# Landmark attention and two feed-forward blocks: V' as eight 64-row tiles, the cosine as one shifted sine, 204 moved deadlines

## The chip, the cores and the metric

The kernel runs on one core of a Trainium2 chip. The core has a matrix engine (TensorE, in the profile PE, with its weight loads as PEld), a vector engine (DVE), an activation engine (ACT), GpSimd (POOL) and a sync engine (SP) whose queue issues the transfers between the chip's memory and SBUF. Matrix products land in PSUM, eight banks of 2 KB in each of 128 partitions; ACT and DVE read it. The metric is the device time of one execution in microseconds (us). TensorE's clock has two levels, 1.2 and 2.4 GHz; the profile's column PEclk gives the granted clock as a share of the higher one.

## The reference

Landmark attention over 4 batches of 8 heads (sequence 576, head size 64, 32 landmarks), then two feed-forward blocks on the 2304 x 512 result:

```python
A  = sm(q, k_lm);  Bm = sm(q_lm, k_lm);  C = sm(q_lm, k)      # sm: scaled scores, softmax
Z  = Bm.T / (norm_1(Bm) * norm_inf(Bm) + 1e-6)
for _ in range(6):
    Z = 2 * Z - Z @ Bm @ Z
x = (A @ Z @ C @ v)                    # heads side by side: [2304, 512]
h = x @ w_in;    g = h * cos(h);       x = g @ w_out           # 512 -> 2048 -> 512
h = x @ w_in2;   g = max(h, 0) + alpha * min(h, 0);  y = g @ w_out2
```

The weights arrive as 64-bit floats; the kernel takes them in as pairs of 32-bit words and rebuilds 32-bit floats on DVE.

## The kernel before, in words

**Attention.** A unit (function `unit`) works on four heads of a batch: loads of k, q and v, transposes on TensorE, landmark sums, scores, softmax. Its result `ah[b, c]` is A transposed, 128 rows (4 heads of 32 landmarks) by 576 columns, split in a high and a low part. `z_path` runs the iteration for Z of two units and ends with W, the 64 x 32 matrix of each of the eight heads by which the first feed-forward weight is folded into the landmarks: V' = W^T w_in, so that h = A V'. W goes through `put` (DVE, L857) into tile `w_`, spread with a mask so that the two heads of a 128-row pair stand in a block diagonal.

**V'.** `vprime(b, fb, c)` makes, for batch b, a slab of 512 of the 2048 columns (fb) and four of the heads (c), one tile of 128 x 512: two products of 128 rows by 64 columns (L885) with 512 streamed columns, into one PSUM bank of the pair called `x`; ACT copies it out (L887, the high part), DVE subtracts for the low part (L888). There are 4 x 4 x 2 = 32 calls. Each 32-bit product stands in the trace as two matmul records.

**Ticks.** `tick(s)` makes a block of 128 rows of h for half a batch (288 columns): 6 matmuls h (L925) into one of two banks `h`; ACT rounds h/2pi to a whole number (L930); DVE forms u = h/2pi - k (L932); ACT takes sin(pi u) (L934) and squares it (L935); DVE forms (1 - 2 sin^2) h (L936), which frees the bank; ACT copies the high part (L939), POOL or DVE subtracts (L323); 12 matmuls (L952) add it to the four `acc` banks. There are 128 ticks.

**Second block.** `btick` does the second feed-forward block, with Strassen products (L1238, L1283) and the closing products (L1319).

**The order** is not written by hand. Every operation is handed to `Plan` with the engines that can do it, a guessed duration and a deadline (`target`); deadlines run backwards through what depends on what. `go` then simulates a run and issues, again and again, the operation that can start earliest, with a small term for the deadline, and the order that it issues is each engine's program:

```python
key = s + KA * min(dl - s, KC)          # KA = 0.004
```

`s` is the planned start and `dl` the deadline, so an offset of 2 us on a deadline moves the key by 0.008 us: it decides only between operations that could start at practically the same moment. `KN` holds the constants, among them PB and AB (a bias for giving work to POOL or ACT) and SW (for switching ACT's function table). `ADJ` adds an offset to a deadline by name: `t105` is every operation of tick 105, `t112:10` its tenth, `y:13` the thirteenth of every `y_load`; u and U are units, z the iteration, v and V are V' calls, c weight conversions, e moves of y1, s, y and o loads of the second block, b its ticks. In the kernel before it is empty. The transfers go into SP's queue in the planned order too, and that queue issues one after the other.

Of the kernel before, what the change touches and what calls it, by code (L numbers as in the profile page):

```python
# [15 lines left out]

WINDOW, WARM = 3.4133, 1.275
INV2PI = 1.0 / (2.0 * math.pi)
KN = dict(T0=46, TA=3.4, TBT=3.05, VE=4.0, U1=-1, U2=36, U3=66, UD=7, UZ=20, C2=48, CD=3.0, LA=4, SW=6.0, BL=0.9, PB=0.2, AB=0.2, LM=126, JG=8, VG=8, AG=8, LW=4, LG=4, KA=0.004, KC=25, DRY=0)

ADJ = {}


class Buf:
# [17 lines left out]
class Plan:  # L42
# [71 lines left out]
    def go(self, free):  # L114
# [9 lines left out]
        for o in self.ops:  # L124
            o.dl += sum(ADJ.get(x, 0.0) for x in o.key)
        ready = {e: [] for e in free}
        seq = {t: [] for t in self.caps}
        dma_free, cur = 0.0, "exp"
        left = len(self.ops)
# [72 lines left out]
        while left:  # L202
            best = None
            for e, lst in ready.items():
                pick = None
                for o in lst:
                    sl = slots(o)
                    if sl is None:
                        continue
                    d = dict(o.engs)[e]  # L210
                    s = max(free[e], o.est, sl)
                    if e == "PE":
                        d = pe_time(s, d)
# [5 lines left out]
                    if len(o.engs) > 1 and any(  # L219
                        max(free[x], o.est, sl) + dx - BIAS.get(x, 0.0) < s + d - BIAS.get(e, 0.0)  # L220
                        for x, dx in o.engs if x != e
                    ):
                        continue
                    key = s + KA * min(dl - s, KC)
                    if pick is None or (key, dl) < pick[0]:
                        pick = ((key, dl), d, o, s)
                if pick and (best is None or pick[3] < best[3]):
                    best = (*pick, e)
            assert best is not None, "no operation can go"
            _, d, o, s, e = best  # L230
            for x, _ in o.engs:
                ready[x].remove(o)
            for b in o.bufs:
                if not b.live:
                    b.live = True
                    seq[b.tag].append(b)
                    b.t = None if KN["DRY"] else b.view(self.place[b.tag][2][(len(seq[b.tag]) - 1) % self.caps[b.tag]])
            o.eng = e
            if e == "PE":
                d = pe_time(s, o.engs[0][1], True)  # L240
            free[e] = s + d
            if o.aset:
                cur = o.aset
            if o.dma:
                dma_free = max(s + 0.65, dma_free) + o.dma
                o.end = dma_free + 0.93
            else:
                o.end = s + d
            if not KN["DRY"]:
                o.fn(e)  # L250
            work = []
            finish(o, work)
            for x in work:
                release(x)
# [4 lines left out]
def kernel(  # L259
# [12 lines left out]
    nc = tc.nc  # L272
# [156 lines left out]
    nc.vector.memset(mask, 0.0)  # L429
    for hh in range(2):  # L430
        nc.vector.memset(mask[64 * hh:64 * hh + 64, hh], 1.0)
    kq = [view([P, 2, 2, 2, M], F32)(at_kq + 32 * M * p) for p in range(NP)]
    for p in range(NP):
        nc.gpsimd.memset(kq[p], 0.0)
    g.held = dict.fromkeys("uUz", [g.buf("zf", lambda _: None)])
    alpha_sb = keep.tile([P, NF], F32, name="alpha_sb")
    kqb = [[g.buf(None) for _ in range(2)] for _ in range(NP)]
    alb = g.buf(None)

# [83 lines left out]
    def unit(u, tu):  # L523
# [72 lines left out]
        if m == 0:  # L596
# [27 lines left out]
            for hh in range(2):  # L624
                sl = slice(64 * hh, 64 * hh + 64)

                def kw(e, sl=sl, hh=hh):
                    o = kq[p][sl, :, :, hh, :]
                    i = pt.t[sl, 0:256].rearrange("p (x y b m) -> p x y b m", x=2, y=2, b=2)[:, :, 0]
                    if e == "ACT":  # L630
                        nc.scalar.activation(o, i, AF.Copy, scale=1.0 / (8.0 * SEG))
                    else:
                        nc.vector.tensor_scalar_mul(o, i, 1.0 / (8.0 * SEG))
                op([dve(128), act(128)], kw, r=[pt], w=[kqb[p][0], kqb[p][1]])
        else:
            for i, t in enumerate((kt, qt)):
# [15 lines left out]
                for hh in range(2):  # L652
                    sl = slice(64 * hh, 64 * hh + 64)

                    def kw(e, sl=sl, hh=hh, i=i, lt=lt):
                        o = kq[p][sl, i, :, hh, :]
                        x = lt.t[sl].rearrange("p (b m) -> p b m", b=2)
                        if e == "ACT":
                            nc.scalar.activation(o, x, AF.Copy, scale=1.0 / (8.0 * SEG))
                        else:  # L660
                            nc.vector.tensor_scalar_mul(o, x, 1.0 / (8.0 * SEG))
                    op([dve2(64), act(64)], kw, r=[lt], w=[kqb[p][i]])

        def scores(dst, ch, which, t, bb, pp):
            n = 64 * (CH[ch][1] - CH[ch][0])
            nc.tensor.matmul(
                out=dst.t[64 * bb:64 * bb + 64, 0:n],
                lhsT=kq[pp][:, which, bb].rearrange("p h m -> p (h m)"),
                rhs=t.t[:, CH[ch][0]:CH[ch][1], bb, :],
            )  # L670

# [85 lines left out]
    def z_path(b, tz):  # L757
# [12 lines left out]
        def pbm(e):  # L770
            for p in range(g0, g0 + n):
                for bb in range(2):
                    for hh in range(2):
                        qd = 2 * bb + hh
                        nc.tensor.matmul(
                            out=pb.t[32 * qd:32 * qd + 32, (p - g0) * M:(p - g0) * M + M],
                            lhsT=kq[p][64 * hh:64 * hh + 64, 1, bb, hh, :],
                            rhs=kq[p][64 * hh:64 * hh + 64, 0, bb, hh, :],
                        )
        op(("PE", 0.134 * n), pbm, r=[x for y in kqb[gs] for x in y], w=[pb])  # L780
        mx, bm, sm, bt = (zs(t + sx, [P, n, w]) for t, w in (("bmx", 1), ("bm", M), ("bsm", 1), ("bt", M)))
# [29 lines left out]
        def icf():  # L811
# [4 lines left out]
        vop(4, lambda e: nv.reciprocal(ic.t, ic.t), rw=[ic])  # L816
        vop(nm_, lambda e: nv.tensor_tensor(bm.t, bm.t, ic.t.to_broadcast([P, n, M]), op=ALU.mult),
            r=[ic], rw=[bm])
        w_ = sb("wt", [P, 2, P])
        c, W = cs[0], M + D  # L820
        heads = [(i, qd, slice(32 * qd, 32 * qd + 32)) for i in range(n) for qd in range(4)]

# [29 lines left out]
        op(("PE", 0.4), wm, r=[y, bm], w=pw)  # L852
        for bb in range(2):
            def put(e, bb=bb):
                o = w_.t[:, :, 64 * bb:64 * bb + 64].rearrange("p i (h m) -> p h i m", h=2)
                x = pw[bb].t[:, 0:n * M].rearrange("p (o i m) -> p o i m", o=1, i=n)
                nv.tensor_tensor(o, x.to_broadcast([P, 2, n, M]), mask.to_broadcast([P, 2, n, M]), op=ALU.mult)  # L857
            vop(128, put, r=[pw[bb]], w=[w_], target=tz)
        for i in range(2):
            wt[b, i] = w_  # L860

    vv, vload = {}, {}

    def vprime(b, fb, c, target):
        g.ctx = f"{'vV'[b > 0]}{2 * fb + c}"
        if b > 1:
            wi = []
            for p in (2 * c, 2 * c + 1):
# [4 lines left out]
                vload.setdefault((b, fb), gates["v"][0])  # L873
                wi.append(f)
        else:
            wi = [wi1[fb, 2 * c], wi1[fb, 2 * c + 1]]
        w_ = wt[b, c]
        pv = psb("x")
        d = vv[b, fb, c] = v_tile()
        valloc.append((b, fb))  # L880

        def v_mm(e):
            for bb in range(2):
                sl = slice(64 * bb, 64 * bb + 64)
                nc.tensor.matmul(out=pv.t[sl], lhsT=w_.t[:, c, sl], rhs=f32(wi[bb].t))  # L885
        op(pe(512, 4), v_mm, r=[w_, *wi], w=[pv, d], target=target)
        op(act(512, True), lambda e: nc.scalar.activation(d.t[:, 0], pv.t, AF.Copy), r=[pv], w=[d], target=target + 0.8)  # L887
        op(dve(512), lambda e: nc.vector.tensor_tensor(d.t[:, 1], pv.t, f32(d.t[:, 0]), op=ALU.subtract),  # L888
           r=[pv], rw=[d], target=target + 1.5)
# [19 lines left out]
    def tick(s):  # L909
# [9 lines left out]
        def h1_mm(e):  # L919
            i = 0  # L920
            for c in range(2):
                vh, vl = vv[b, fb, c].t[:, 0], vv[b, fb, c].t[:, 1]
                xh, xl = ah[b, c][0].t, ah[b, c][1].t
                for w_, x in ((vh, xh), (vh, xl), (vl, xh)):
# [14 lines left out]
        op(act(CW), lambda e: nc.scalar.activation(gh.t, hc.t, AF.Copy), r=[hc], w=[gh, gl])  # L939
        op([pool(CW), dve(CW)], lambda e: sub(e, gl.t, hc.t, f32(gh.t)), r=[hc, gh], w=[gl])  # L940
# [50 lines left out]

    def vgroup(b, fbs):
        for fb in fbs:
            for c in range(2):
                vprime(b, fb, c, tick_time(vfirst[b, fb]) - KN["VE"])

    FH = JG // 4
    vgroup(0, range(FH))
# [386 lines left out]
```

## Time and profile before

| what | value |
|---|---|
| median of 3 runs | 875.13 us (874.53 to 878.24) |
| profiled execution | 876.8 us, of which the span of its records is 875.0 us |
| TensorE busy | 823.1 us, 94% of the span |
| VectorE busy | 642.5 us, 73% |
| ScalarE busy | 475.9 us, 54% |
| GpSimd busy | 200.0 us, 23% |
| moved by DMA | 103.28 MB |

A busy share is an average over parts with different limits. The span has a first part in which loads and conversions feed the first ticks, a long part of ticks with the attention of later batches among them, a short change-over to the second block, and the second block itself. Where TensorE is busy all the time, the end moves only with TensorE's own work; where it waits, with what it waits for.

### The profile page before, as it was taken

Reading aid. Unit: us, or ns where it says so; the run is one execution under the profiler, and the core shown is the slowest. Engines: PE = TensorE matmul, PEld = TensorE weight load, DVE = VectorE, ACT = ScalarE, POOL = GpSimd, SP = SyncE. Lnnn points to the kernel's source line nnn. Section 1 sums busy time; section 2 is a strip of 40 time slices with the busy share of each in tenths; the row PEclk is TensorE's granted clock in tenths of the full one; section 3 lists DMA queues with packets and bytes.
Section 4 is the critical chain, followed back from the end, with each engine's and each line's share of the span. In section 5 each row is a group of like instructions: output and inputs, shape, how many; then the busy total and the mean of one; then the engine's idle time right before and its main releaser. Section 6 shows DMA issues by size and latency. Waiting matters only on the chain.

```text
span 875.0 us, 16117 instructions
## 1 busy us (share of the span) xinstructions
PE 823.1 (94%) x6065; PEld 721.5 (82%) x6065; DVE 642.5 (73%) x1296; ACT 475.9 (54%) x1085; POOL 200.0 (23%) x221
## 2 busy tenths in 40 slices
PE   6658899999999999998999889999999999999997
PEld 4337678889788878877899779899999999999996
DVE  5978979986986789777978999865665566555563
ACT  4357647787866678566876443443344324433431
POOL 0325402334431332122511332200220012000110
PEclk9788799999999999999999999999999999999999
DMA  9474716676266935455463322130113011310231
GB/s 234 144 200 122 180 30 219 198 181 137 89 208 200 226 101 157 165 189 169 133 207 110 112 78 85 60 105 25 37 61 86 25 37 61 85 37 25 70 111 24
DMA packets 87901, 103.28 MB, mean 118 GB/s; under 512 B 35856, under 2 KB 62992, under 8 KB 87824
## 3 DMA queue, kind: packets, MB, share of 16 engines
q1 hardware_dynamic: 87824, 102.27, 40.6%
q8 instruction: 47, 0.77, 0.4%
q14 instruction: 30, 0.25, 0.1%
HBM read 79.96 MB, written 22.28 MB: 117 GB/s over the span
## 4 chain that ended last, share of the span: by engine, by line
PE 66%; DVE 15%; DMA 10%; ACT 3%; issue 3%; SPq 1%; DVEq 0%; ACTq 0%
PE acc L1319 20%; PE acc L952 14%; PE h L1238 9%; PE h L925 7%; PE x L1238 7%; DMA m<-in_moe_w_in_dram 5%; DVE m L323 3%; DMA m<-in_moe_w_out_dram 3%; PE x L885 2%; DVE m L469 1%; PE h L1283 1%; PE x L1283 1%; DVE m L471 1%; DMA m<-wi2d 1%; DVE m L936 1%
## 5 line engine op out<-in xcount | busy, mean ns | idle before, releaser
L952 PE MATMUL acc<-m,m 128*128 128x288 f32 x1536 | 239.1, 302 | 2.7 <-DVE m L323 2.2
L323 POOL TENSOR_TENSOR m<-m,m 128x288 fp32r<-128x288 f32 (+4 forms) x126 | 125.3, 1000 | 444.6 <-ACT m L939 193.3
L952 PEld LDWEIGHTS acc<-m,m 128*128 128x128 f32 x1536 | 214.8, 191 | 13.5 <-issue 5.5
L1319 PE MATMUL acc<-m,m 128*128 128x512 f32 x864 | 207.6, 391 | 0.7 <-DVE m L323 0.4
L323 DVE TENSOR_TENSOR m<-m,m 128x512 fp32r<-128x512 f32 (+3 forms) x274 | 174.0, 659 | 30.2 <-ACT m L1160 7.4
L1319 PEld LDWEIGHTS acc<-m,m 128*128 128x128 f32 x864 | 158.9, 189 | 31.5 <-DVE m L323 0.9
L925 PE MATMUL h<-m,m 128*128 128x288 f32 x768 | 131.2, 307 | 12.5 <-DVE m L936 11.1
L925 PEld LDWEIGHTS h<-m,m 128*128 128x128 f32 x768 | 110.7, 193 | 29.1 <-DVE m L936 18.6
L1238 PE MATMUL h<-m,m 128*128 128x256 f32 x768 | 107.8, 284 | 4.0 <-ACT m L318 4.0
L1307 ACT ACTIVATE m<-m 128x512 fp32r<-128x512 f32 (+1 forms) x80 | 46.3, 588 | 111.8 <-DVE m L1305 109.4
L1238 PEld LDWEIGHTS h<-m,m 128*128 128x128 f32 x768 | 101.0, 192 | 7.1 <-ACT m L318 4.8
L1238 PE MATMUL x<-m,m 128*128 128x256 f32 x576 | 80.9, 286 | 1.8 <-ACT m L318 1.8
L939 ACT ACTIVATE m<-m 128x288 fp32r<-128x288 f32 x128 | 56.2, 441 | 45.1 <-DVE m L936 41.3
L1261 DVE TENSOR_TENSOR m<-h,m 128x512 f32<-128x512 f32 x32 | 22.1, 690 | 78.1 <-ACT m L318 77.9
L1238 PEld LDWEIGHTS x<-m,m 128*128 128x128 f32 x576 | 74.0, 191 | 3.4 <-ACT m L318 2.0
L936 DVE SCALAR_TENSOR_TENSOR m<-m,h 128x288 f32<-128x288 f32 x128 | 56.8, 445 | 24.1 <-ACT m L935 23.8
L318 ACT ACTIVATE m<-h 128x256 f32<-128x256 f32 (+3 forms) x90 | 35.5, 395 | 63.2 <-PE h L1238 57.3
L930 ACT ACTIVATE m<-h 128x288 int32<-128x288 f32 x128 | 51.8, 406 | 31.8 <-PE h L925 30.9
L934 ACT ACTIVATE m<-m 128x288 f32<-128x288 f32 x128 | 55.7, 441 | 24.0 <-DVE m L932 23.4
L1071 ACT ACTIVATE m<-m 128x512 fp32r<-128x512 f32 x68 | 41.3, 627 | 45.2 <-PE h L1238 19.0
L932 DVE SCALAR_TENSOR_TENSOR m<-h,m 128x288 f32<-128x288 f32 x128 | 57.3, 448 | 6.2 <-ACT m L930 5.5
L935 ACT ACTIVATE m<-m 128x288 f32<-128x288 f32 x128 | 55.5, 439 | 2.3
(143 smaller groups left out, 864.8 us busy)
## 6 DMA issues: line engine op xcount, KB each, us to landing
m<-in_moe_w_in_dram SPq DMA_DIRECT2D x32, 512.0 KB, 4.9
m<-wi2d SPq DMA_DIRECT2D x56, 256.0 KB, 3.2
m<-in_moe_w_out_dram SPq DMA_DIRECT2D x24, 512.0 KB, 4.7
m<-w1d SPq DMA_DIRECT2D x32, 256.0 KB, 5.7
y1d<-m SPq DMA_DIRECT2D x24, 288.0 KB, 2.9
out_dram<-m SPq DMA_DIRECT2D x36, 128.0 KB, 2.4
w1d<-m SPq DMA_DIRECT2D x16, 256.0 KB, 5.6
wi2d<-m SPq DMA_DIRECT2D x16, 256.0 KB, 2.8
```

The source lines that it names most:

```text
L323: ENG[e].tensor_tensor(o, a, b, op=ALU.subtract)
L925: nc.tensor.matmul(out=hp.t[:, 0:CW], lhsT=w_[:, js], rhs=x[:, cs], start=(i == 0), stop=(i == 5))
L930: op(act(CW, True), lambda e: nc.scalar.activation(k_.t, hp.t[:, 0:CW], AF.Copy, scale=INV2PI), r=[hp], w=[k_], target=T + 0.8)
L932: op(dve(CW), lambda e: nc.vector.scalar_tensor_tensor(u.t, hp.t[:, 0:CW], INV2PI, k_.t, op0=ALU.mult, op1=ALU.subtract), r=[hp, k_], w=[u])
L934: op(act(CW), lambda e: nc.scalar.activation(u.t, u.t, AF.Sin, scale=math.pi), rw=[u], aset="sin")
L935: op(act(CW), lambda e: nc.scalar.activation(u.t, u.t, AF.Square, scale=math.sqrt(2.0)), rw=[u])
L936: op(dve(CW), lambda e: nc.vector.scalar_tensor_tensor(hc.t, u.t, 1.0, hp.t[:, 0:CW], op0=ALU.subtract, op1=ALU.mult, reverse0=True), r=[h ...
L939: op(act(CW), lambda e: nc.scalar.activation(gh.t, hc.t, AF.Copy), r=[hc], w=[gh, gl])
L952: nc.tensor.matmul(out=yg[o].t[:, 0:CW], lhsT=w_.t[:, sl], rhs=x.t, start=(j == ja and i == 0), stop=(j == jb and i == 2),)
L1238: nc.tensor.matmul(out=rv(k), lhsT=a_.t[:, p, c2, js], rhs=b_.t[:, q_, c2, 0:hw], start=(first and c2 == 0 and i == 0), stop=(c2 == 1 and ...
L1307: op(act(w), lambda e, m_=m_, gh=gh: nc.scalar.activation(gh.t[:, 0:w], m_.t[:, 0:w], AF.Copy), r=[m_], w=[gh, gl])
L1319: nc.tensor.matmul(out=ya[n][t].t, lhsT=gv(x_), rhs=r_.t, start=(st and k == 0), stop=(en and k == 2))
```

## The change

Three things are changed. V' is made for all eight heads at once: 16 calls instead of 32, each with eight products of 64 rows by 32 columns, into both `x` banks; W is kept without the mask, and the landmark tiles `kq` are laid out so that the heads of odd units are swapped, which puts the eight products in eight different places of the array. The cosine is sin(2 pi u + pi/2), with k rounded after adding 0.25, so the squaring falls away and the last DVE operation is a plain product. And the planner has new constants, a scale for each engine's durations, and 204 offsets in `ADJ`.

```diff
-KN = dict(..., SW=6.0, BL=0.9, PB=0.2, AB=0.2, ..., KC=25, DRY=0)
-ADJ = {}
+KN = dict(..., SW=6.582, BL=0.9, PB=0.058, AB=0.1901, ..., KC=18.8859, DRY=0, PS=1.0002, AS=1.0, DS=0.9985, GS=0.9577, MS=1.0, ML=0.65, MD=0.939)
+ADJ = {
+    "U2:21": 0.67, "U3:4": 2.78, "U5": 0.25, "U5:14": -0.75, "U5:48": 1.66, "U6": 2.12, "U7:1": -3.84,
...
+    "z:19": 1.22, "z:2": 0.44, "z:26": 2.97, "z:27": 3.22, "z:28": 1.88, "z:33": -0.54, "z:6": -0.79, "z:8": 1.1,
+}
+        scale = {"PE": KN["PS"], "ACT": KN["AS"], "DVE": KN["DS"], "POOL": KN["GS"], "SP": 1.0}
-                    d = dict(o.engs)[e]
+                    d = dict(o.engs)[e] * scale[e]
-                dma_free = max(s + 0.65, dma_free) + o.dma
-                o.end = dma_free + 0.93
+                dma_free = max(s + KN["ML"], dma_free) + o.dma * KN["MS"]
+                o.end = dma_free + KN["MD"]
-    kq = [view([P, 2, 2, 2, M], F32)(at_kq + 32 * M * p) for p in range(NP)]
+    kq = [view([P, 2, 4, M], F32)(at_kq + 32 * M * p) for p in range(NP)]
+    quarter = keep.tile([P, 1], F32, name="quarter")
+    nc.vector.memset(quarter, math.pi / 2)
...
-        w_ = sb("wt", [P, 2, P])
+        w_ = sb("wt", [P, 2, 2, M])
             def put(e, bb=bb):
-                o = w_.t[:, :, 64 * bb:64 * bb + 64].rearrange("p i (h m) -> p h i m", h=2)
-                x = pw[bb].t[:, 0:n * M].rearrange("p (o i m) -> p o i m", o=1, i=n)
-                nv.tensor_tensor(o, x.to_broadcast([P, 2, n, M]), mask.to_broadcast([P, 2, n, M]), op=ALU.mult)
-            vop(128, put, r=[pw[bb]], w=[w_], target=tz)
+                copy(e, w_.t[:, :, bb], pw[bb].t[:, 0:n * M].rearrange("p (i m) -> p i m", i=n))
+            op([dve(64), act(64, True)], put, r=[pw[bb]], w=[w_], target=tz)
-    def vprime(b, fb, c, target):
+    def vprime(b, fb, target):
...
-        pv = psb("x")
-        d = vv[b, fb, c] = v_tile()
+        pv, d = [psb("x") for _ in range(2)], [v_tile() for _ in range(2)]
         def v_mm(e):
-            for bb in range(2):
-                sl = slice(64 * bb, 64 * bb + 64)
-                nc.tensor.matmul(out=pv.t[sl], lhsT=w_.t[:, c, sl], rhs=f32(wi[bb].t))
+            for c in range(2):
+                for bb in range(2):
+                    for hh in range(2):
+                        qd = 2 * bb + (hh ^ c)
+                        sl = slice(64 * hh, 64 * hh + 64)
+                        nc.tensor.matmul(
+                            out=pv[c].t[32 * qd:32 * qd + 32], lhsT=w_.t[sl, c, bb], rhs=f32(wi[2 * c + bb].t)[sl])
...
-        op(act(CW, True), lambda e: nc.scalar.activation(k_.t, hp.t[:, 0:CW], AF.Copy, scale=INV2PI),
+        op(act(CW, True), lambda e: nc.scalar.activation(k_.t, hp.t[:, 0:CW], AF.Copy, scale=INV2PI, bias=0.25),
-        op(act(CW), lambda e: nc.scalar.activation(u.t, u.t, AF.Sin, scale=math.pi), rw=[u], aset="sin")
-        op(act(CW), lambda e: nc.scalar.activation(u.t, u.t, AF.Square, scale=math.sqrt(2.0)), rw=[u])
-        op(dve(CW), lambda e: nc.vector.scalar_tensor_tensor(
-            hc.t, u.t, 1.0, hp.t[:, 0:CW], op0=ALU.subtract, op1=ALU.mult, reverse0=True), r=[hp, u], w=[hc],
+        op(act(CW), lambda e: nc.scalar.activation(u.t, u.t, AF.Sin, scale=2.0 * math.pi, bias=quarter), rw=[u], aset="sin")
+        op(dve(CW), lambda e: nc.vector.tensor_tensor(hc.t, u.t, hp.t[:, 0:CW], op=ALU.mult), r=[hp, u], w=[hc],
```

## Rows read from the trace of the kernel before

**Rows 1.** The page's busy times: engine, busy us, share of the span, instructions.

```profile
PE 823.1 (94%) x6065; PEld 721.5 (82%) x6065; DVE 642.5 (73%) x1296; ACT 475.9 (54%) x1085; POOL 200.0 (23%) x221
```

**Rows 2.** Busy time in four parts of the span, then in one short stretch.

```profile
0.00:110.00 110.00, 79.15 (x660) 57.41 (x661) 86.35 (x185) 62.80 (x135) 34.59 (x44) 0.84 0.68 176
110.00:440.00 330.00, 320.81 (x2717) 278.11 (x2716) 265.27 (x593) 233.09 (x554) 101.44 (x117) 0.99 0.55 161
440.00:560.00 120.00, 113.56 (x752) 105.85 (x753) 106.21 (x197) 63.33 (x144) 30.98 (x24) 0.97 0.33 106
560.00:875.00 315.00, 309.57 (x1941) 280.14 (x1940) 184.64 (x324) 116.64 (x256) 33.00 (x36) 1.00 0.20 58
...
30.00:40.00 10.00, 4.00 (x98) 2.67 (x91) 9.35 (x21) 2.05 (x3) 4.55 (x4) 0.69 0.77 210
```

**Rows 3.** TensorE's waits over the span: us in total, times, longest.

```profile
PE h L925 <- DVE m L936: 11.1, 13, 2.6
PE h L613 <- DMA m<-in_k_dram: 5.9, 1, 5.9
PE h L1238 <- ACT m L318: 4.0, 3, 2.3
PE h L826 <- DVE m L839: 3.8, 4, 1.6
PE x L885 <- DVE m L471: 3.6, 2, 3.2
...
PE x L1238 <- ACT m L318: 1.8, 1, 1.8
```

**Rows 4.** Timeline around one V' slab: start us, length, what.

```profile
417.88 1.94 PE L885 MATMUL x<-m,m 128*64 128x512 f32 x8
...
419.74 1.06 PE L925 MATMUL h<-m,m 128*128 128x288 f32 x6
```

**Rows 5.** V' records alone: that slab in 0.04 us steps, then one long stretch.

```profile
417.90:417.94 0.04, 0.04 (x2) 0.04 (x4) 1.00 0.00 0
...
418.34:418.38 0.04, 0.04 (x4) 0.02 (x2) 1.00 0.00 0
...
110.00:440.00 330.00, 27.12 (x112) 6.78 (x112) 0.99 0.55 161
```

**Rows 6.** A step of the iteration for Z: timeline, then its matmuls in 0.02 us.

```profile
358.02 0.53 PE L826 MATMUL x<-m 32*32 32x96 f32 x16
358.48 1.06 PE L952 MATMUL acc<-m,m 128*128 128x288 f32 x6
...
358.02:358.04 0.02, 0.02 (x4) 0.02 (x4) 1.00 0.00 0
```

**Rows 7.** Timeline: products in four column places, and in stacked rows.

```profile
26.91 0.90 PE L711 MATMUL h<-m,m 128*32 128x64 f32 x40
27.74 0.55 PE L590 MATMUL h<-m,m 128*128 128x128 f32 x3
...
38.58 0.32 PE L851 MATMUL h<-m 32*64 32x32 f32 x2 [1.90 <-DVE m L844]
38.59 0.32 PE L851 MATMUL x<-m 32*64 32x32 f32 x2
```

**Rows 8.** Groups by line on ACT and DVE: busy us, mean ns, idle before.

```profile
L935 ACT ACTIVATE m<-m 128x288 f32<-128x288 f32 x128 | 55.5, 439 | 2.3
...
L887 ACT ACTIVATE m<-x 128x512 fp32r<-128x512 f32 x32 | 18.4, 588 | 7.7 <-PE x L885 7.6
...
L888 DVE TENSOR_TENSOR m<-x,m 128x512 fp32r<-128x512 f32 x32 | 21.5, 683 | 3.1 <-ACT m L887 3.0
L936 DVE SCALAR_TENSOR_TENSOR m<-m,h 128x288 f32<-128x288 f32 x128 | 56.8, 445 | 24.1 <-ACT m L935 23.8
L972 DVE TENSOR_TENSOR m<-acc,m 128x288 f32<-128x288 f32 x16 | 6.9, 452 | 1.2 <-PE acc L952 0.9
```

**Rows 9.** Waits of SP's queue, up to 480 us: in total, times, longest.

```profile
SPq L494 <- DVE m L471: 117.0, 22, 20.1
```

More of the change, by code (lines that the diff above doesn't have):

```diff
@@ L18 @@
 INV2PI = 1.0 / (2.0 * math.pi)
-KN = dict(T0=46, TA=3.4, TBT=3.05, VE=4.0, U1=-1, U2=36, U3=66, UD=7, UZ=20, C2=48, CD=3.0, LA=4, SW=6.0, BL=0.9, PB=0.2, AB=0.2, LM=126, JG=8, VG=8, AG=8, LW=4, LG=4, KA=0.004, KC=25, DRY=0)
-ADJ = {}
+KN = dict(T0=46, TA=3.4, TBT=3.05, VE=4.0, U1=-1, U2=36, U3=66, UD=7, UZ=20, C2=48, CD=3.0, LA=4, SW=6.582, BL=0.9, PB=0.058, AB=0.1901, LM=126, JG=8, VG=8, AG=8, LW=4, LG=4, KA=0.004, KC=18.8859, DRY=0, PS=1.0002, AS=1.0, DS=0.9985, GS=0.9577, MS=1.0, ML=0.65, MD=0.939)
+ADJ = {
[27 rows of a table added]
+}
 class Buf:
@@ L220, in go @@
                         max(free[x], o.est, sl) + dx - BIAS.get(x, 0.0) < s + d - BIAS.get(e, 0.0)
-                        for x, dx in o.engs if x != e
+                        for x, dx in ((y, dy * scale[y]) for y, dy in o.engs) if x != e
                     ):
@@ L239, in go @@
             if e == "PE":
-                d = pe_time(s, o.engs[0][1], True)
+                d = pe_time(s, o.engs[0][1] * scale[e], True)
             free[e] = s + d
@@ L627, in kw @@
                 def kw(e, sl=sl, hh=hh):
-                    o = kq[p][sl, :, :, hh, :]
-                    i = pt.t[sl, 0:256].rearrange("p (x y b m) -> p x y b m", x=2, y=2, b=2)[:, :, 0]
+                    o = kq[p][sl, :, 1:3] if c and hh == 0 else kq[p][sl, :, 0:4:3] if c else kq[p][sl, :, hh:4:2]
+                    i = pt.t[sl, 0:256].rearrange("p (x y b m) -> p y b x m", x=2, y=2, b=2)[:, 0]
                     if e == "ACT":
@@ L655, in kw @@
                     def kw(e, sl=sl, hh=hh, i=i, lt=lt):
-                        o = kq[p][sl, i, :, hh, :]
+                        o = kq[p][sl, :, 2 * i + (hh ^ (c * (1 - i)))]
                         x = lt.t[sl].rearrange("p (b m) -> p b m", b=2)
@@ L667, in scores @@
                 out=dst.t[64 * bb:64 * bb + 64, 0:n],
-                lhsT=kq[pp][:, which, bb].rearrange("p h m -> p (h m)"),
+                lhsT=kq[pp][:, bb, 2 * which:2 * which + 2].rearrange("p h m -> p (h m)"),
                 rhs=t.t[:, CH[ch][0]:CH[ch][1], bb, :],
@@ L776, in pbm @@
                             out=pb.t[32 * qd:32 * qd + 32, (p - g0) * M:(p - g0) * M + M],
-                            lhsT=kq[p][64 * hh:64 * hh + 64, 1, bb, hh, :],
-                            rhs=kq[p][64 * hh:64 * hh + 64, 0, bb, hh, :],
+                            lhsT=kq[p][64 * hh:64 * hh + 64, bb, 2 + hh],
+                            rhs=kq[p][64 * hh:64 * hh + 64, bb, hh ^ (p - g0)],
                         )
@@ L854, in put @@
             def put(e, bb=bb):
-                o = w_.t[:, :, 64 * bb:64 * bb + 64].rearrange("p i (h m) -> p h i m", h=2)
-                x = pw[bb].t[:, 0:n * M].rearrange("p (o i m) -> p o i m", o=1, i=n)
-                nv.tensor_tensor(o, x.to_broadcast([P, 2, n, M]), mask.to_broadcast([P, 2, n, M]), op=ALU.mult)
-            vop(128, put, r=[pw[bb]], w=[w_], target=tz)
-        for i in range(2):
-            wt[b, i] = w_
+                copy(e, w_.t[:, :, bb], pw[bb].t[:, 0:n * M].rearrange("p (i m) -> p i m", i=n))
+            op([dve(64), act(64, True)], put, r=[pw[bb]], w=[w_], target=tz)
+        wt[b] = w_
     vv, vload = {}, {}
-    def vprime(b, fb, c, target):
-        g.ctx = f"{'vV'[b > 0]}{2 * fb + c}"
+    def vprime(b, fb, target):
+        g.ctx = f"{'vV'[b > 0]}{fb}"
         if b > 1:
             wi = []
-            for p in (2 * c, 2 * c + 1):
+            for p in range(NP):
                 f = sb("wi", [P, 512], I32)
@@ L875, in vprime @@
         else:
-            wi = [wi1[fb, 2 * c], wi1[fb, 2 * c + 1]]
-        w_ = wt[b, c]
-        pv = psb("x")
-        d = vv[b, fb, c] = v_tile()
-        valloc.append((b, fb))
-        def v_mm(e):
-            for bb in range(2):
-                sl = slice(64 * bb, 64 * bb + 64)
-                nc.tensor.matmul(out=pv.t[sl], lhsT=w_.t[:, c, sl], rhs=f32(wi[bb].t))
[L886 to L889, printed above, removed]
+            wi = [wi1[fb, p] for p in range(NP)]
+        w_ = wt[b]
+        pv, d = [psb("x") for _ in range(2)], [v_tile() for _ in range(2)]
+        valloc.extend([(b, fb)] * 2)
+        def v_mm(e):
+            for c in range(2):
[5 more added lines that the diff above has]
+                            out=pv[c].t[32 * qd:32 * qd + 32], lhsT=w_.t[sl, c, bb], rhs=f32(wi[2 * c + bb].t)[sl])
+        op(pe(512, 4), v_mm, r=[w_, *wi], w=[*pv, *d], target=target)
+        for c in range(2):
+            vv[b, fb, c] = d[c]
+            op(act(512, True), lambda e, c=c: nc.scalar.activation(d[c].t[:, 0], pv[c].t, AF.Copy), r=[pv[c]],
+               w=[d[c]], target=target + 0.8)
+            op(dve(512), lambda e, c=c: nc.vector.tensor_tensor(
+                d[c].t[:, 1], pv[c].t, f32(d[c].t[:, 0]), op=ALU.subtract), r=[pv[c]], rw=[d[c]], target=target + 1.5)
     JG = KN["JG"]
@@ L993, in vgroup @@
         for fb in fbs:
-            for c in range(2):
-                vprime(b, fb, c, tick_time(vfirst[b, fb]) - KN["VE"])
+            vprime(b, fb, tick_time(vfirst[b, fb]) - KN["VE"])
     FH = JG // 4
```

25 rows, old and new, of the table ADJ are left out of this document.

## The prediction

> **What bounds the kernel now.** I read the page's busy times first: TensorE is busy 823.1 of 875.0 us [rows 1], so it waits 51.9 us in all, and no other engine comes near it. Then the span in four parts [rows 2]. In the first 110 us TensorE is busy 79.15 us at a mean granted clock of 0.84; as the clock has two levels, 0.84 means that some 35 us of the 110 ran at 1.2 GHz. DVE is busy 86.35 us there and the DMA engines 0.68 of the time: this part is fed by loads and conversions, and an example is 30 to 40 us, with TensorE at 4.00, DVE at 9.35 and a clock of 0.69. From 110 to 440 us TensorE is busy 320.81 of 330 and waits 9.2 us: here the end moves by what TensorE itself has less to do, plus those 9.2. From 440 to 560 it waits 6.4 us beside a DVE that is busy 106.21 of 120. From 560 on it is busy 309.57 of 315; the change takes no work out of that part. Last I read what TensorE waits for [rows 3]: 11.1 us in 13 waits on L936, the operation that gives a tick's `h` bank back; 5.9 us for the first load, which nothing here touches; the others are waits on ACT or DVE for work that stood behind other work, 13.2 us for the four that are shown.
>
> **V' in eight tiles.** A slab today is two calls. At the full clock its eight matmul records start at 417.88 and the next product starts at 419.74 [rows 4]: 1.86 us. In the fine steps two records run at once, and the next two join at 418.34 [rows 5], about 0.44 us after the first: four rounds of two, 4 x 0.44, and some 0.1 at the edges. After the change a slab is eight products, sixteen records of the same 512 columns, in eight places (two halves of the rows, four column groups). If all eight places run at once, these are two rounds: 2 x 0.44 and 0.15 to 0.2 for edges and starts, about 1.05 us; 0.8 us less. Of the 16 slabs 14 (112 records of eight a slab) lie between 110 and 440 us [rows 5], where TensorE is the bound: 14 x 0.8 = 11.2. The other two lie in the first part; at 0.8 each they would save 1.6, but conversions and loads set the pace there, so I take 1.0 for both. Together 12.2 us.
>
> Do eight run at once? No row shows it at 512 columns. For it: in the iteration for Z sixteen records of 96 columns take from 358.02 to 358.48, and four stand side by side in the first 0.02 us, in four different row groups and all into one PSUM bank [rows 6]; by the V' round a record of 96 columns costs 0.44 x 96 / 512 = 0.083 us, so one after the other they would take 1.32 us. And L851 starts two records into bank h and two into bank x within 0.01 us [rows 7], of which pairs lie on the same columns and different rows. Against it: four column places of the same rows, L711, give 40 records in 0.83 us [rows 7], 0.021 us each, where one alone would cost 0.44 x 64 / 512 = 0.055: only 2.6 at once. These are short records and their weight loads may set that pace, but taken as it stands, V' would run 2 x 2.6 at once: 16 x 0.44 / 5.2 + 0.14 = 1.5 us, a gain of 0.36 a slab, 5.4 in all with 14 slabs and 0.4 for the first two. I take the full 12.2, since 0.44 us records give the loads ample time; the bounds are 0 and 16 x 0.93 = 14.9, half of today's slabs.
>
> The Trainium skill, page "TensorEngine Tiling (Array Packing)", section "Restrictions and Gotchas", speaks against this change: it says that different row tiles cannot access the same PSUM bank at the same time. Rows 6 show four row groups writing one bank side by side, so this trace does not bear the rule out as a limit on their speed.
>
> What goes with V': ACT copies (588 ns) and DVE subtractions (683 ns) stay 32 each [rows 8]. A slab now holds both `x` banks from its first matmul to the last subtraction, 1.05 + 0.59 + 2 x 0.68 = 3.0 us, where each call held one bank for some 0.95 + 0.59 + 0.68 = 2.2. Queued behind it for these banks are the transposes and scores of the attention of later batches; what hides the wait is the ticks' own matmuls, which use the `h` and `acc` banks. I take nothing, and price it below. A slab also needs its four weight tiles at once; this matters for the second slab, which already waited for L471 [rows 3]. `put` loses its mask product and can go to ACT: eight operations, each below the 0.45 us of a 288-column one, at the end of the chain of Z with ticks beside it in three of four cases; nothing, 3.6 us at most. The new layout of `kq` changes addresses only.
>
> **The cosine.** 128 squarings of 439 ns leave ACT, 56 us of its 475.9 [rows 8, 1]. ACT isn't the bound; what counts is that an `h` bank comes back one ACT operation earlier. The 13 waits on L936 sum to 11.1 us [rows 3]. Each gets shorter by at most 0.44, so by at most 5.7; some are shorter than that, and I take 4.5. The bounds are 0 (ACT's next operation in the queue takes the place, and the wait with it) and 11.1 (with ACT lighter, all of them go). The last DVE step becomes a plain product of an SBUF and a PSUM operand; the nearest row is L972, 452 ns against 445 [rows 8], so 0.9 us more of DVE, under TensorE's work. The biases on the rounding and the sine have no row; operations of that size on ACT differ by less than the 439 ns that leave, so ACT gets lighter either way. One memset more on DVE lies in the wait for the first load.
>
> **The order.** The offsets are mostly under 4 us, so the key moves by under 0.02 us: they settle ties, but one settled tie changes all that follows, so no step can be followed singly, and every queue, SP's too, gets a somewhat different order. I bound it by the waits. What another order can remove are waits on an engine that was doing something else: the 13.2 us shown, and 6.6 of L936 that the cosine leaves, 19.8 together. What it can cost: new waits of the size of those present, and the longest three here are 3.2, 2.6 and 2.3 us [rows 3], 8.1. Between 8 lost and 20 won I take 10 won: DVE, the engine behind most of these waits, has 14 us of slack even between 440 and 560 us [rows 2], so its queue can be ordered better, but the loads of the first part can't be made faster. A lower bias for POOL gives DVE some more subtractions; the room for them is the same.
>
> **Sum.** 876.8 us for the profiled execution, less 12.2, 4.5 and 10: 850.1. That execution was 1.7 above the median of the runs shown (875.13), so I forecast 848.4.
>
> **Rivals.**
> *V' does not run eight at once.* With 5.2 at once as L711 suggests the sum gives 855; with no gain from V' 860.6 (848.4 + 12.2). For it speaks L711, against it rows 6 and the longer records. 6 in 100.
> *The row halves exclude each other in a bank.* Neighbouring records then alternate between the halves in one bank and run one by one: 16 x 0.44 = 7.0 us a slab, 5.2 more than now, 83 us in sixteen slabs, and no 12.2: 848.4 + 12.2 + 83 = 944. By the Trainium skill's rule named above it would be this. Rows 6 speak plainly against it: 2 in 100.
> *A store ahead of loads in SP's queue* (the other side). The queue issues one after the other; a store of a converted tile waits for its last DVE step, up to 20.1 us in one of 22 waits [rows 9], and the loads behind it wait too. Today the loads behind come soon enough. If the new order sets the ticks' weight loads behind two such stores, TensorE stands for 2 x 20.1: 889. It decides from 26.7 us on, all that I expect to be gained. For it speaks that every queue is reordered, against it that the planner simulates this queue. 6 in 100.
> *Both `x` banks held.* If each of 14 slabs costs TensorE 2 us of its 3.0, that is 28, and the time is 876, no change; from 1.9 us a slab it eats the gain. Against it speak the ticks' other banks. 4 in 100.
> *The order gives back.* With 8 lost in place of 10 won, 866: 8 in 100.
> *The order wins more than its bound,* since waits in the first part also bring the lower clock: below 834. 4 in 100.
>
> **How the numbers follow.** 70 in 100 are left for the forecast; with V' at 10 to 14, the waits of L936 at 1 to 6 and the order at 0 to 20 it lies between 835 and 864. The range 834 to 866 takes in the rival with V' at less and most of that in which the order gives back. About 0.5%, 4.4 us, is what a measurement can tell from no change. Faster: 70 + 6 + 8 + 4 = 88. No change: the 4 of the `x` banks. Slower: 2 + 6 = 8.
>
> **What would show it.** V': sixteen records a slab in two rounds, some 1.0 us to the next product, 16 such slabs. One round per record would show the exclusion, four rounds no gain. Cosine: L935 gone, ACT near 420 us, the waits on the operation that frees `h` at half of 11.1. Order: TensorE's idle time, 51.9 now, near 37, above all in the first 110 us and from 440 to 560; the part from 560 on as long as now, about 315 us. The prediction is wrong if the idle time stays near 52 or grows, or if the records of V' do not start together.

## The result, and the profile after

The changed kernel takes 862.43 us (median of 4 runs, 861.33 to 865.76) against 875.43 us: a ratio of 0.9835, 95% interval 0.9808 to 0.9862, 13 to 14 us less. That lies in the range that was given (834 to 866), at its slow end; the forecast was 848.4, twice the gain.

Busy times of the changed kernel, in the columns of [rows 1]:

```profile
PE 808.0 (94%) x6193; PEld 716.6 (83%) x6193; DVE 640.9 (74%) x1296; ACT 439.4 (51%) x971; POOL 199.9 (23%) x208
```

TensorE is busy for 15.1 us less. The products of V' make up 13.1 of them; their lines before and after, with busy us, mean ns, and the idle time just before them:

```profile
L885 PE MATMUL x<-m,m 128*64 128x512 f32 x128 | 34.8, 641 | 3.8 <-DVE m L471 3.6 <-DVE m L857 0.2
```

```profile
L915 PE MATMUL x<-m,m 64*32 64x512 f32 x256 | 21.7, 647 | 1.6 <-DVE m L502 1.6
```

Its idle time is 860.5 - 808.0 = 52.5 us, where it was 51.9; the forecast had put it near 37. So over the whole span the gain is busy time that TensorE no longer has, and in sum no waiting went away.

Its time in four parts (the last ends with the shorter span), beside [rows 2]:

```profile
0.00:110.00 110.00, 80.34 (x703) 60.14 (x703) 88.57 (x194) 60.74 (x133) 35.69 (x45) 0.86 0.67 176
110.00:440.00 330.00, 316.18 (x2876) 281.91 (x2875) 268.69 (x598) 210.09 (x473) 98.06 (x110) 0.99 0.57 169
440.00:560.00 120.00, 116.30 (x775) 107.65 (x775) 108.41 (x204) 59.49 (x131) 34.89 (x22) 1.00 0.30 96
```

TensorE waits 29.7 us in the first part (30.9 before), 13.8 from 110 to 440 us (9.2 before) and 3.7 from 440 to 560 (6.4 before). The forecast saw waits going away above all in the first and the third of these parts, where they shrank by 1.2 and 2.7 us; they grew by 4.6 in the middle one, where it took TensorE as the bound. These are equal times, not equal work. The first Strassen product, which stands behind the last h product of the ticks, shows how far the kernel got. Its line in the kernel before and after: duration, first and last start.

```profile
L1238 PE MATMUL h<-m,m x768: 276/281/463, 477.1 to 814.7; 128*128 128x256 f32 x192
```

```profile
L1269 PE MATMUL h<-m,m x768: 277/281/387, 467.2 to 799.2; 128*128 128x256 f32 x192
```

9.9 us are won by 467 us and 5.6 more by the last of these starts. The second block, from the first of these starts to the end, in the kernel before and after:

```profile
477.10:875.00 397.90, 386.03 (x2414) 348.89 (x2412) 261.53 (x456) 151.21 (x325) 58.00 (x54) 0.99 0.21 62
```

```profile
467.20:860.50 393.30, 384.29 (x2414) 347.32 (x2412) 261.48 (x456) 151.60 (x328) 64.21 (x51) 1.00 0.22 63
```

So of the 14.5 us between the two executions 9.9 come off the part of the ticks and 4.6 off the second block, to which neither V' nor the cosine belongs: there TensorE waits 9.0 us in place of 11.9 and is busy for 1.7 less.

V' did what it was made for. One slab on the timeline, and then its records in steps of 0.04 us, beside [rows 4, 5]:

```profile
377.22 1.09 PE L915 MATMUL x<-m,m 64*32 64x512 f32 x16
378.24 0.67 PE L984 MATMUL acc<-m,m 128*128 128x288 f32 x3
```

```profile
377.26:377.30 0.04, 0.04 (x8) 0.04 (x16) 1.00 0.65 230
...
377.62:377.66 0.04, 0.04 (x8) 0.00 (x0) 1.00 0.84 307
...
377.70:377.74 0.04, 0.04 (x16) 0.00 (x0) 1.00 2.06 486
```

Eight records run together, the second eight join 0.45 us later, and the next product starts 1.02 us after the first record; before it was 1.86.

The cosine, and the product that gives `h` back, beside [rows 8]; then TensorE's longest waits, beside [rows 3]:

```profile
L968 ACT ACTIVATE m<-m,quarter 128x288 f32<-128x288 f32 x128 | 67.5, 533 | 32.8 <-DVE m L966 31.9
...
L969 DVE TENSOR_TENSOR m<-m,h 128x288 f32<-128x288 f32 x128 | 56.9, 446 | 14.7 <-ACT m L968 13.9
```

```profile
PE h L959 <- DVE m L969: 12.5, 13, 3.3
PE h L644 <- DMA m<-in_k_dram: 6.0, 1, 6.0
PE h L857 <- DVE m L870: 4.2, 4, 1.5
PE x L636 <- DVE m L633: 2.7, 2, 1.8
PE x L1269 <- ACT m L347: 2.7, 3, 1.1
PE h L959 <- DVE m L922: 2.4, 1, 2.4
```

The sine takes 533 ns. In the kernel before its line, L934, stands at 441:

```profile
L934 ACT ACTIVATE m<-m 128x288 f32<-128x288 f32 x128 | 55.7, 441 | 24.0 <-DVE m L932 23.4
```

By the lengths of its operations the chain of a tick got shorter by 439 - 92 = 347 ns, and yet the waits for an `h` bank did not shrink: 12.5 us in 13 waits, 11.1 in 13 before.

What the longest of them, 3.34 us from 422.4 on, consists of is on the timelines of TensorE, of DVE, and of POOL beside it:

```profile
425.73 1.49 PE L959 MATMUL h<-m,m 128*128 128x288 f32 x5 [3.34 <-DVE m L969]
```

```profile
419.21 4.70 DVE L352 TENSOR_TENSOR m<-m,m 128x288 fp32r<-128x288 f32 x5
423.83 0.44 DVE L966 SCALAR_TENSOR_TENSOR m<-h,m 128x288 f32<-128x288 f32 x1
```

```profile
417.22 6.41 POOL L352 TENSOR_TENSOR m<-m,m 128x256 f32<-128x256 f32 x7
```

Five subtractions stand in DVE's queue ahead of L966, an earlier step of the tick whose L969 TensorE waits for. They take 0.94 us each while POOL works beside them; one by itself takes 0.45 (at 403.00 in the kernel with V' alone, below). In the whole trace of the change, 54 of the 73 such subtractions on DVE have no two-tensor operation (TENSOR_TENSOR) of POOL beside them and take 418 to 461 ns; the other 19 take 441 to 1542. The planner counts such a subtraction as 288 / 960 + 0.07 = 0.37 us. For one by itself that is right, since the records of neighbouring DVE operations overlap by some 0.08 us (L324 at 399.63 and L470 at 401.06, below); what it leaves out is POOL.

### The profile page after: what moved, and what is told of

It is laid out like the page before. It is cut to its first block, busy times and chain, and to the rows that moved or that the text cites. A ratio compares the mean times of both kernels' runs of the same rounds, so it can differ in the third digit from the quotient of the medians.

```text
span 860.5 us, 16346 instructions
## 1 busy us (share of the span) xinstructions
PE 808.0 (94%) x6193; PEld 716.6 (83%) x6193; DVE 640.9 (74%) x1296; ACT 439.4 (51%) x971; POOL 199.9 (23%) x208
## 4 chain that ended last, share of the span: by engine, by line
PE 64%; DVE 18%; DMA 11%; ACT 3%; issue 2%; SPq 1%; POOL 1%; DVEq 0%; ACTq 0%; POOLq 0%
PE acc L1350 22%; PE acc L984 12%; PE h L1269 10%; PE x L1269 7%; DMA m<-in_moe_w_in_dram 6%; PE h L959 6%; DVE m L352 3%; DVE m L502 2%; DVE m L500 2%; DMA m<-in_moe_w_out_dram 2%; DVE m L969 2%; PE x L1314 1%; PE h L1314 1%; DVE m L966 1%; DVE m L498 1%
## 5 line engine op out<-in xcount | busy, mean ns | idle before, releaser
L352 POOL TENSOR_TENSOR m<-m,m 128x288 fp32r<-128x288 f32 (+3 forms) x114 | 121.3, 1071 | 474.8 <-ACT m L971 225.9
L352 DVE TENSOR_TENSOR m<-m,m 128x512 fp32r<-128x512 f32 (+4 forms) x286 | 172.7, 626 | 38.5 <-ACT m L1102 14.5
L959 PE MATMUL h<-m,m 128*128 128x288 f32 x768 | 130.4, 307 | 15.3 <-DVE m L969 12.5
L968 ACT ACTIVATE m<-m,quarter 128x288 f32<-128x288 f32 x128 | 67.5, 533 | 32.8 <-DVE m L966 31.9
L347 ACT ACTIVATE m<-h 128x256 f32<-128x256 f32 (+4 forms) x94 | 36.8, 391 | 63.6 <-PE h L1269 55.1
L966 DVE SCALAR_TENSOR_TENSOR m<-h,m 128x288 f32<-128x288 f32 x128 | 57.3, 449 | 14.3 <-ACT m L964 14.0
L969 DVE TENSOR_TENSOR m<-m,h 128x288 f32<-128x288 f32 x128 | 56.9, 446 | 14.7 <-ACT m L968 13.9
L1336 DVE SCALAR_TENSOR_TENSOR m<-m,m 128x512 f32<-128x512 f32 x64 | 47.6, 785 | 0.0
```

Source lines behind the costliest of these rows:

```text
L352: ENG[e].tensor_tensor(o, a, b, op=ALU.subtract)
L959: nc.tensor.matmul(out=hp.t[:, 0:CW], lhsT=w_[:, js], rhs=x[:, cs], start=(i == 0), stop=(i == 5))
L966: op(dve(CW), lambda e: nc.vector.scalar_tensor_tensor(u.t, hp.t[:, 0:CW], INV2PI, k_.t, op0=ALU.mult, op1=ALU.subtract), r=[hp, k_], w=[u])
L969: op(dve(CW), lambda e: nc.vector.tensor_tensor(hc.t, u.t, hp.t[:, 0:CW], op=ALU.mult), r=[hp, u], w=[hc], target=T + 2.6)
L1336: op(dve(w), lambda e, m_=m_, hv=hv: nc.vector.scalar_tensor_tensor(m_.t[:, 0:w], hv(), 0.0, m_.t[:, 0:w], op0=ALU.max, op1=ALU.add), r=hr ...
```

## The experiments

Two readings stood against each other. By the first the parts are worth their work: V' some 12 us, the cosine a few, the order the rest. By the second the tick part is held up as much by what stands where in the in-order queues of DVE and ACT as by TensorE, so that each edit lets the planner draw another order, and the draw decides. Ratios are to the kernel before, which ran beside each; one hundredth is 8.75 us.

**V' alone, the cosine alone, both with the old planner.** Three kernels: the kernel before with only the V' part of the diff; with only the cosine; and with both, the constants and the empty offsets of before:

```diff
-KN = dict(..., SW=6.582, ..., PB=0.058, AB=0.1901, ..., KC=18.8859, ..., PS=1.0002, DS=0.9985, GS=0.9577, ..., MD=0.939)
-ADJ = {"U2:21": 0.67, ...}
+KN = dict(..., SW=6.0, ..., PB=0.2, AB=0.2, ..., KC=25, ..., PS=1.0, DS=1.0, GS=1.0, ..., MD=0.93)
+ADJ = {}
```

> The kernel before with V' in eight tiles alone; old cosine, old planner constants, no offsets. Theory A (each part is worth its own work, the order adds little): sixteen records a slab, 1.1 us a slab, 14 x 0.8 = 11 to 12 us less, so 863 to 865. Rival B (holding both x banks costs what the tiles win): TensorE's waits grow by 5 or more and the time is 868 to 875. Rival C (every edit gives the planner another order, and that alone moves the time by some us either way): 858 to 870, with TensorE's idle time off by up to 5 us and no wait on the x banks among the long ones.

> The kernel before with the shifted sine alone. Theory A (an h bank comes back 0.35 us earlier: the squaring's 0.44 less the 0.09 that the sine now takes longer): the 13 waits on the operation that frees h sum to 7 to 8 us in place of 11.1 and the time is 871 to 873. Rival B (these waits are set by the queue of DVE, not by the length of the chain): waits of 10 to 13 us, 874 to 877. Rival C (another order by chance): anything from 870 to 880 with the idle time to match.

> The changed kernel with V' and the cosine, but the planner's constants and the empty offsets of before. Theory A (the offsets win next to nothing beyond another order): 859 to 866. Rival B (the offsets win the 10 us that were forecast, and the new structure costs as much elsewhere): 870 to 874, with TensorE's idle time at 60 or more. If the offsets do harm: below 859.

Measured: V' alone 1.0082 (1.0051 to 1.0114), 7 us slower; the cosine alone 1.0030 (1.0013 to 1.0047); both 1.0002 (0.9986 to 1.0018). V' alone lies outside all three ranges given for it. With the cosine alone the waits on `h` are 13.2 us in 14, not the 7 to 8 of its theory A. The step from both with the old planner to the change is 0.0167, 14.6 us. So with the planner's plain order the two edits won nothing, and the new constants and offsets together won all. (The offsets without the constants follow below; the constants without the offsets were not run.) V' alone and its longest waits:

```profile
PE 810.8 (92%) x6193; PEld 716.0 (81%) x6193; DVE 649.5 (74%) x1301; ACT 475.5 (54%) x1093; POOL 192.0 (22%) x210
```

```profile
PE h L929 <- DVE m L940: 21.7, 21, 3.7
PE h L614 <- DMA m<-in_k_dram: 6.1, 1, 6.1
PE h L1241 <- ACT m L319: 4.9, 4, 2.9
PE x L885 <- DVE m L472: 3.9, 2, 2.9
...
PE x L591 <- DVE m L892: 3.6, 2, 1.9
```

TensorE is busy for 12.3 us less, about what V' was forecast to save, and waits 881.1 - 810.8 = 70.3 us, 18.4 more. The waits for `h` doubled, 10.6 us more. The rival of the two `x` banks is there, as two waits for V's last subtraction (L892) of 3.6 us in all, but it is the small part. One of the 21, 2.60 us, on TensorE's timeline and then on DVE's and POOL's:

```profile
402.16 1.30 PE L929 MATMUL h<-m,m 128*128 128x288 f32 x6 [2.60 <-DVE m L940]
```

```profile
399.05 0.66 DVE L468 TENSOR_SCALAR m<-m 128x512 int32<-128x512 int32 x1 [1.46 <-DMA m<-in_moe_w_in_dram]
399.63 1.51 DVE L324 TENSOR_TENSOR m<-m,m 128x288 fp32r<-128x288 f32 x1
401.06 0.68 DVE L470 SCALAR_TENSOR_TENSOR m<-m,m 128x512 int32<-128x512 int32 x1
401.67 0.44 DVE L940 SCALAR_TENSOR_TENSOR m<-m,h 128x288 f32<-128x288 f32 x1
...
403.00 0.45 DVE L324 TENSOR_TENSOR m<-m,m 128x288 fp32r<-128x288 f32 x1
```

```profile
398.12 2.70 POOL L1102 TENSOR_TENSOR m<-m,m 128x512 f32<-128x512 f32 x2
```

DVE first stands still for 1.46 us for a load of weights, then takes two steps of their conversion and, between them, a subtraction that lasts 1.51 us beside POOL's sums, and only then L940, which TensorE waits for.

**V' twice, in the change's own order.** The durations that the planner is given stay, so nothing moves:

```diff
-            for c in range(2):
+            for c in (0, 1, 0, 1):
                 for bb in range(2):
```

> The changed kernel in its own order, with the eight products of each V' slab issued twice (the second time over the first): TensorE's V' work is back at about what it was before the change, and nothing else in the order changes. Theory A (in a fixed order TensorE's work is worth its full length): 14 slabs x 0.85 and a little for the first two, 12 more, 873 to 876. Rival B (the work saved turns into waits for DVE, in whose queue conversions stand ahead of the ticks, so that it is worth little even in a fixed order): 863 to 868, and TensorE's idle time falls from 52.5 us by what its busy time gains.

Measured: 0.9945 (0.9923 to 0.9967), 0.0110 or 9.6 us more than the change. A slab is 1.88 us to the next product, and the busy times are:

```profile
383.98 1.95 PE L915 MATMUL x<-m,m 64*32 64x512 f32 x32
385.86 0.67 PE L984 MATMUL acc<-m,m 128*128 128x288 f32 x3
```

```profile
PE 818.3 (94%) x6449; PEld 719.0 (83%) x6449; DVE 642.6 (74%) x1296; ACT 440.3 (51%) x971; POOL 200.4 (23%) x208
```

TensorE's busy time grew by 10.3 us, its idle time is 51.9 us, 52.5 in the change. The line of V' grew by 13.5 us, from 21.7 to 35.2. The first Strassen product starts at 476.8, where it stood before the change (477.1), and the second block lasts 393.4 us, as in the change. So in this order, held, V' is worth 9.6 us (the two intervals leave some 3 us either way): most of its 13.5, four fifths of the 12.2 forecast. The median, 872.02, lies between the ranges of the two theories, 1 us below that of A.

**A copy behind each sine, in the change's own order.**

```diff
             nc.scalar.activation(u.t, u.t, AF.Sin, scale=2.0 * math.pi, bias=quarter)
+            nc.scalar.activation(u.t, u.t, AF.Copy)
```

> The changed kernel in its own order, with a plain copy in place behind every sine on ScalarE (0.44 us, as the squaring was): the chain of a tick is as long as before the change and nothing else in the order changes. Theory A (the cosine's shorter chain is worth what was forecast in a fixed order): waits on the operation that frees the h bank 4 us or more longer, 867 to 872. Rival B (ScalarE's gain is hidden): 861 to 865.

Measured: 1.0096 (1.0070 to 1.0122), 0.0261 or 23 us more than the change. The copy's line, and the wait:

```profile
L970 ACT ACTIVATE m<-m 128x288 f32<-128x288 f32 x128 | 57.1, 446 | 4.1
```

```profile
PE h L959 <- DVE m L972: 24.2, 28, 3.5
```

Waits for `h` went from 13 to 28 and from 12.5 to 24.2 us, and TensorE's idle time from 52.5 to 69.5. The copy lengthens the chain and also gives ACT 53 us more work; the run doesn't tell the two apart. An order that was made for the short chain doesn't bear the long one; both theories had put it far lower. This doesn't say that the square was worth 23 us in the kernel before, whose order was planned with it: with the old planner, the cosine alone won nothing.

**Orders by chance.** Offsets at the same 204 names, dealt out anew at random: for the kernel before, and, at half the size, for the new work with the old constants. Then the change's offsets as they are, for the new work with the old constants, and for the kernel before:

```diff
-ADJ = {"U2:21": 0.67, "U3:4": 2.78, ...}
+ADJ = {...}          # the same names; the same offsets (or half of them) in another order
```

> The kernel before, old V' and old cosine, with the 204 offsets dealt out anew at random among their names: one order by chance for the old work. Theory A (the plain order of before was a lucky draw among orders by chance, so that V' alone met a worse draw): 880 to 895. Rival B (orders by chance differ little and the loss of 6 us with V' alone is the structure's): 872 to 879.

> V' and the cosine as changed, the planner's constants of before, and at the same 204 names offsets of half the size, dealt out anew at random: one more order by chance for the new work. Theory A (an order by chance costs what the plain one costs, and only chosen offsets win): 872 to 885. Rival B (any offsets are as good, the plain order was an unlucky one): 860 to 870.

> The new V' and cosine with the 204 offsets of the change, but the planner's constants of before (SW, PB, AB, KC and the scales). Theory A (offsets and constants were found as one set for one order, and with other constants the greedy planner takes another path early, so the offsets mean nothing): a time among the orders by chance, 876 to 885. Rival B (the offsets carry the win by themselves, operation by operation): 861 to 867.

> The kernel before, old V' and cosine and constants, with the 204 offsets as they are in the change. Theory A (they fit one order of the new work alone): an order by chance for the old work, 877 to 888. Rival B (they correct deadlines that were wrong in the old kernel too): 862 to 870.

Measured: 1.0110 (1.0084 to 1.0136), 1.0082 (1.0057 to 1.0107), 1.0040 (1.0012 to 1.0067) and 1.0051 (1.0026 to 1.0077). None of the four is fast, and the median of each (885.55, 883.19, 881.88 and 881.78 us) lies in the range of its theory A. Their busy times, in the same sequence:

```profile
PE 824.6 (93%) x6065; PEld 718.0 (81%) x6065; DVE 643.1 (73%) x1297; ACT 476.4 (54%) x1091; POOL 201.0 (23%) x216
```

```profile
PE 818.9 (93%) x6193; PEld 722.2 (82%) x6193; DVE 643.9 (73%) x1291; ACT 442.2 (50%) x969; POOL 197.0 (22%) x215
```

```profile
PE 814.9 (92%) x6193; PEld 719.3 (81%) x6193; DVE 641.6 (73%) x1282; ACT 443.1 (50%) x972; POOL 204.5 (23%) x223
```

```profile
PE 827.4 (93%) x6065; PEld 723.6 (82%) x6065; DVE 645.5 (73%) x1294; ACT 470.2 (53%) x1085; POOL 202.5 (23%) x221
```

Three orders that nobody chose for the old work (the kernel before, 1; 1.0110; 1.0051) and three for the new (1.0002; 1.0082; 1.0040) have means of 1.0054 and 1.0041 and spread by 0.011 and 0.008. With spans of 875.0, 882.9, 885.2 and of 875.1, 884.5, 883.3, TensorE is idle for 51.9, 58.3 and 57.8 us with the old work and 63.5, 65.6 and 68.4 with the new (for 875.1 the busy time is 811.6). Each is one execution, and those of 884.5, 883.3 and 885.2 were 3 to 5 us above the median of their kernel. In these six orders, what TensorE no longer does, it waits.

With the new work, the change's offsets win nothing without its constants. What the constants win by themselves, and what both would do for the old work, was not run. The last of the four doesn't replace that: a tick of the old work has one operation more and V' twice the calls, so some of the names mean other operations there. Yet a part of what the offsets do carries over. The second block with both edits in the planner's plain order, then in the last and the third of the four:

```profile
476.50:875.10 398.60, 386.26 (x2414) 348.79 (x2412) 259.67 (x450) 152.59 (x328) 60.19 (x55) 0.99 0.21 62
```

```profile
491.70:885.20 393.50, 384.31 (x2414) 347.42 (x2412) 257.36 (x439) 151.23 (x329) 69.34 (x61) 0.99 0.22 63
```

```profile
478.10:883.30 405.20, 390.03 (x2414) 351.40 (x2412) 261.59 (x441) 151.87 (x329) 71.32 (x65) 0.99 0.21 61
```

With the old work the offsets bring the second block to 393.5 us, as in the change (393.3), from 397.9; it is the part of the ticks that they make longer, 491.7 us in place of 477.1. With the new work and the old constants they make the second block longer, 405.2.

**The sine without its bias operand.** The quarter turn moves into DVE's step, W carries 1/2pi, and the product takes it back; the operations and their order are those of the change:

```diff
-nc.scalar.activation(k_.t, hp.t[:, 0:CW], AF.Copy, scale=INV2PI, bias=0.25)
-nc.vector.scalar_tensor_tensor(u.t, hp.t[:, 0:CW], INV2PI, k_.t, op0=ALU.mult, op1=ALU.subtract)
-nc.scalar.activation(u.t, u.t, AF.Sin, scale=2.0 * math.pi, bias=quarter)
-nc.vector.tensor_tensor(hc.t, u.t, hp.t[:, 0:CW], op=ALU.mult)
+nc.scalar.activation(k_.t, hp.t[:, 0:CW], AF.Copy, bias=0.25)
+nc.vector.scalar_tensor_tensor(u.t, k_.t, 0.25, hp.t[:, 0:CW], op0=ALU.subtract, op1=ALU.subtract)
+nc.scalar.activation(u.t, u.t, AF.Sin, scale=-2.0 * math.pi)
+nc.vector.scalar_tensor_tensor(hc.t, u.t, 2.0 * math.pi, hp.t[:, 0:CW], op0=ALU.mult, op1=ALU.mult)
```

> The changed kernel with its order, but the sine without a bias operand: the quarter turn goes into the DVE step before it, W carries the factor 1/2pi and the product takes it back. Same values, same number of operations. Theory A (the operand costs ScalarE the 0.09 us by which the sine grew from 441 to 533 ns, and the ticks' chain feels it): sine at 441 ns, ScalarE 428 us, the waits on the operation that frees h down by 1 to 3 us, 859 to 861. Rival B (the chain's length isn't what these waits hang on): sine at 441 ns, same waits, 861.5 to 863.5.

> The changed kernel once more, beside the next one: 861 to 863.5 by every theory.

> The changed kernel with the sine free of its bias operand, on the same chip as the one before. Theory A (in a fixed order the length of a tick's chain counts, as the copy behind the sine showed with 22 us for 0.44 us of length): 0.09 us less a tick gives up to 22 x 0.09 / 0.44 = 4.5, and 1 to 4 are expected, 858 to 862. Rival B (a shorter chain than the order was made for is worth nothing): 862 to 863.5.

Measured: 0.9815 (0.9791 to 0.9840) in the first run; then, side by side, the change 0.9841 (0.9809 to 0.9873) and this 0.9791 (0.9761 to 0.9821), medians of 865.01 and 860.47 us. The sine in the last run:

```profile
L970 ACT ACTIVATE m<-m 128x288 f32<-128x288 f32 x128 | 55.8, 441 | 32.6 <-DVE m L968 31.8
```

The 92 ns are gone. It was the faster both times, by 0.0020 and 0.0050 (2 and 4 us), but the intervals of the pair overlap a little: it is likely faster than the change, and clearly faster than the kernel before. That the shorter chain is the cause isn't shown. The waits on `h` in the pair, the change first:

```profile
PE h L959 <- DVE m L969: 12.4, 12, 3.4
```

```profile
PE h L961 <- DVE m L971: 12.7, 13, 3.3
```

They are the same, as rival B of the first run had it. Of the 6.7 us between the two profiled executions (864.0 and 857.3) 6.2 are busy time of TensorE, 810.5 and 804.3, at mean granted clocks of 0.972 and 0.978.

## Why the prediction was right, and where it wasn't

**V'.** The step was right: two rounds of eight, 1.02 us a slab against 1.05 forecast, and rows of both halves in one bank side by side, so the limit to 2.6 column places at once (the rival from L711) and the exclusion in a bank are both refuted for these products. The Trainium skill, "TensorEngine Tiling (Array Packing)", section "Restrictions and Gotchas", says that different row tiles cannot access the same PSUM bank at the same time; here four products, two of each half of the rows, wrote four different quarters of a bank's partitions together, and eight ran in two banks at full pace. Its price, 12.2, is 9.6 in the order of the change.

**The cosine.** The mechanism was named with a wrong size on both sides. The chain got 0.347 us shorter, not 0.44, since the sine's bias tile costs 92 ns. The Trainium skill, "ScalarE: Activation LUTs", section "What ACT_TABLE_LOAD costs", says that each pointer operand adds about 93 ns; the trace agrees. The prediction had found no row for the biases and left them out of the chain. And that 13 waits each get shorter, by at most 0.44, is not how it works: the waits for `h` are 13 again and sum to 12.5. What the cosine is worth by itself stays open: nothing in the plain order, and the 23 us of the copy are what it cost to upset a chosen order.

**The sum.** This is the step that failed: 876.8 less 12.2, 4.5 and 10, as if the path stayed and the parts came off it one by one. They don't, for the order is drawn anew with every edit. With the planner's plain order V' and the cosine together are worth nothing (0.2 us slower), not 16.7; the order, bounded at 20 and put at 10, is worth 14.6. The terms come to 14 and not to 26.7. That the total fell into the range, at its slow end, is luck: two terms were too large and one too small. Of the order's 14.6 us 5.3 lie in the second block (398.6 to 393.3), which the prediction expected to last as long as before. And to take TensorE as the bound from 110 to 440 us was too simple a reading of 320.81 busy of 330: DVE, busy 265.27 there, works through an in-order queue with load conversions and subtractions ahead of the ticks' steps, and when TensorE needs less, that queue can set the pace. That TensorE then waits more is shown by its idle time in three orders of each kind; that DVE's queue is what stands behind most of these waits is read from the traces, not tested by taking work from DVE. In the order of the change, where V' issued twice costs 9.6 us, TensorE's own work does set the pace for most of its length.

**The rivals.** TensorE waits for a load twice, 6.0 us for the first and 1.2, so nothing like the 40 us priced for stores in SP's queue came. The transposes wait for V's last subtraction, which gives an `x` bank back, once:

```profile
PE x L621 <- DVE m L922: 0.7, 1, 0.7
```

The price set on both banks held, 28 us, was far off. An idle time that stays near 52 us was a sign by which the prediction would call itself wrong; it is 52.5.

What stays open is what a chosen order would do for the old work: the four orders above and the plain ones say only that unchosen ones lie between 1.000 and 1.011 whatever the work. So how much of the 13 us the new work made possible, and how much the search, isn't told apart.

## What to carry to other kernels

Where a planner or a compiler orders the work anew after each edit, judge an edit twice: in a held order (double the work or add the old step without telling the planner) and over several orders drawn by chance. An engine at 97% need not be the only bound when another at 80% works through an in-order queue: look at what stands in that queue ahead of the operation that is waited for. A gain of one per cent from an edit can't be told from a new draw unless several draws are run.

## What the runs showed that was not expected

The old work in its plain order and in one with random offsets of at most 6 us differs by 1.1%. A chain longer by 0.45 us in an order made for a shorter one cost 23 us in 128 ticks. And DVE's subtraction of two SBUF operands, 288 columns, takes 0.45 us by itself and 0.94, once 1.51, beside two-tensor operations of POOL. The Trainium skill, "GPSIMD Engine Reference", section "Specifications", says that POOL shares its SBUF interfaces with DVE and that they contend when a DVE instruction has two SBUF inputs; the trace agrees, though some beside POOL are as short as 441 ns. The planner's guess of 0.37 us has no room for that.
